# Gathering a chunk's decay rows on ScalarE and moving them by DMA, in a gated linear attention fused with a maxout layer

## The chip, the cores and the metric

The kernel runs on one core of a Trainium2 chip. The core has a matrix engine (TensorE, PE in the profile), VectorE (DVE), ScalarE (ACT), GpSimd (POOL) and SyncE (SP), which here only issues DMA transfers. Each engine works through its own instruction list in order; they meet through semaphores. The metric is the device time of one execution in microseconds (us), median of several runs.

## What is computed

Two stages, one after the other. The first is a recurrence per batch entry and head with a state of 48x48 and a decay per state row; the second is a maxout layer on its output.

```
B, H, S, D = q.shape                      # 4, 8, 768, 48
f = 1.0 / (1.0 + np.exp(-f_logit))
state = np.zeros((B, H, D, D)); y = np.zeros_like(q)
for t in range(S):
    state = f[:, :, t, :, None] * state + np.einsum('bhd,bhe->bhde', k[:, :, t], v[:, :, t])
    y[:, :, t] = np.einsum('bhd,bhde->bhe', q[:, :, t], state)
x = y.transpose(0, 2, 1, 3).reshape(B * S, H * D)          # 3072 x 384
out = np.maximum(x @ w1, x @ w2) @ w_out                   # d_ff = 1024
```

All inputs and the output are float32 in HBM.

## The kernel before

The sequence is cut into 6 chunks of 128 positions. A *tile* is one chunk of one batch entry with all 8 heads, 128 positions by 384 columns; there are 24, and tile `i` is chunk `i // 4` of batch entry `i % 4`. Within a chunk the recurrence is written with cumulative sums of the log decay: with `ell = log(1 + exp(-f_logit))`, a matmul with an upper triangular matrix gives `cum`, the sum of `ell` from the chunk's start to each position (L214). Then `ei = exp(cum)` scales k into `kp` (L237, VectorE), `ed = exp(-cum)` scales q into `qp` (L242, GpSimd). The scores of a chunk are `qp` times `kp`, masked (`a`, `am`); the output `y` of a tile is the state of the chunk before, multiplied by `qp` (L307), plus the scores times v (L312).

The state of the next chunk is `(state + sum of kp times v)`, times the decay over the whole chunk. The sum is the matmul `sa` (L281), `tmp` adds the old state on VectorE (L289), and `st` multiplies with the decay on GpSimd (L296), as two instructions of 64 partitions, one for the even heads (partitions 0 to 63), one for the odd (64 to 127). Heads are handled in 4 pairs; a head takes 48 of its 64 partitions.

The decay over the chunk, `fl`, must lie along the *partitions* of the state, whereas `cum` has the positions on its partitions and the head's rows along its columns. So the kernel before sums `ell` once more, with `ell` as the stationary operand: four matmuls, one per pair of heads, of 128x1 with a column of ones (L216), into columns 384 to 387 of the same PSUM tile. `a_fl` (L232) is a ScalarE activation of 128x4 that gives `fl = exp(-sum)`. The last chunk hands no state on and leaves out L216, `fl`, `sa`, `tmp` and `st`.

The second stage: `y` is copied to `x` (L317), transposed (`xT`), and with `d = x @ (w1 - w2)` in two halves (`d0`, `d1`, L334) and `g = relu(d)` in two halves (`g0`, `g1`, L341, called `gT`), the output is `o = x @ (w2 @ w_out) + g @ w_out`, as `o0` (6 of the 11 matmuls) and `o1` (the other 5) at L352. Of `o1`, the first matmul needs the first half of `g`, the four others the second half. `ob` evicts it and `out` stores it.

Every instruction's place is written out by hand in three strings of words "operation, tile": a prologue, a step that is repeated, and an epilogue. In a step for tile `i` the number is added to `i`:

```
st -4  d0 -1  cum 1  a 0  ed 1  d1 -1  g0 -1  am 0  lv 2  qp 1  fl 1  ei 1  lq 3  g1 -1
o0 -1  kpv 1  y 0  tmp -2  lk 3  o1 -1  x 0  e 2  xT 0  tr 1  ln 2  out -4  xTe 0  sa -1
tre 1  ob -1  lf 4  v 1
```

The order on one engine is the order of its words. So in the step of tile 12 GpSimd does `st` of tile 8 and then `qp` of tile 13; ScalarE does `ed`, `g0`, `fl`, `ei`, `g1`, `x`, `e`, `ln`; SyncE issues the loads `lv` 14, `lq` 15, `lk` 15, the store `out` 8 and the load `lf` 16. All DMA transfers are issued by SyncE and go into one queue. Each of the loads `lf`, `lk`, `lq`, `lv` (L148) fetches 192 KB as 1024 pieces of 192 bytes, into one of 9 buffers for its kind. `y` of tile 12 reads the state that `st` of tile 8 has written. `tmp` has two buffers, `fl` has five; `cum`, `tr`, `sa`, `y` and `xT` share three PSUM buffers.

The functions that the change touches:

Of the kernel before, what the change touches and what calls it, by code (L numbers as in the profile page):

```python
# [10 lines left out]
F32 = mybir.dt.float32  # L11
BF16 = mybir.dt.bfloat16
AF = mybir.ActivationFunctionType
# [25 lines left out]
"""  # L39

STEP = """
st -4  d0 -1  cum 1  a 0  ed 1  d1 -1  g0 -1  am 0  lv 2  qp 1  fl 1  ei 1  lq 3  g1 -1
o0 -1  kpv 1  y 0  tmp -2  lk 3  o1 -1  x 0  e 2  xT 0  tr 1  ln 2  out -4  xTe 0  sa -1
tre 1  ob -1  lf 4  v 1
"""
FIRST_STEP = 7
EPILOGUE = """
st 15  d0 18  cum 20  a 19  ed 20  d1 18  g0 18  am 19  qp 20  ei 20  lv 21  g1 18  o0 18
tmp 17  st 16  out 15  y 19  kpv 20  o1 18  x 19  lk 22  e 21  xT 19  tr 20  ln 21  xTe 19
# [14 lines left out]
def kernel(  # L64
# [13 lines left out]
    nc = tc.nc  # L78
    B, H, S, D = q.shape
    C = 128  # L80
    nch = S // C
    dm = H * D
# [3 lines left out]
    DP = 64  # L86
    NP = H // 2
# [3 lines left out]
    consts = ctx.enter_context(tc.tile_pool(name="consts", bufs=1))  # L91
    loads = ctx.enter_context(tc.tile_pool(name="loads", bufs=9))
    work = ctx.enter_context(tc.tile_pool(name="work", bufs=2))
# [8 lines left out]
    qp_b = [consts.tile([C, H, DP], BF16, name=f"qp{n}") for n in range(NQ)]  # L102
    kp_b = [consts.tile([C, H, DP], BF16, name=f"kp{n}") for n in range(NQ)]
    ell_b = [consts.tile([C, H, DP], BF16, name=f"ell{n}") for n in range(2)]
    st_b = [[consts.tile([C, NP, 2 * D], BF16, name=f"st{b}_{n}") for n in range(2)] for b in range(B)]
    ut = consts.tile([C, C], BF16)
    ident = consts.tile([C, C], BF16)
    ones_col = consts.tile([C, 1], BF16)
# [10 lines left out]
    def setup(n):  # L119
        if n == 0:  # L120
            for t in ell_b:
                nc.vector.memset(t, 0.0)
            nc.vector.memset(ones_col, 1.0)
            make_upper_triangular(nc, ut, 1.0, diag=True)
            make_identity(nc, ident)
            for t in (kp_b[0], qp_b[0]):
                nc.vector.memset(t, 0.0)
        elif n == 1:
            nc.vector.tensor_copy(mask, ut.unsqueeze(1).to_broadcast([C, H, C]))
            for t in kp_b[1:] + qp_b[1:]:  # L130
                nc.vector.memset(t, 0.0)
        else:
            for b in range(B):
                for t in st_b[b]:
                    nc.gpsimd.memset(t, 0.0)
# [3 lines left out]
    st = {}  # L139
# [37 lines left out]
    psum = {}  # L177
# [33 lines left out]
    def p_cum(i):  # L211
        ell = st[i]["ell"]
        ps = psum["cum", i] = ps_s.tile([C, 512], F32, name="cum", tag="s")
        nc.tensor.matmul(out=ps[:, 0:dm], lhsT=ut, rhs=ell[:, :, 0:D], start=True, stop=True)  # L214
        for p in range(NP if i // B < nch - 1 else 0):
            nc.tensor.matmul(out=ps[:, dm + p:dm + p + 1],  # L216
                             lhsT=ell[:, 2 * p:2 * p + 2, :].rearrange("p h d -> p (h d)"),
                             rhs=ones_col, start=True, stop=True)
# [7 lines left out]
        nc.scalar.activation(t, psum["cum", i][:, 0:dm], AF.Exp, scale=-1.0)  # L226

    def a_fl(i):
        if i // B == nch - 1:
            return  # L230
        t = st[i]["fl"] = work.tile([C, NP], F32, name="fl", tag="fl", bufs=5)
        nc.scalar.activation(t, psum["cum", i][:, dm:dm + NP], AF.Exp, scale=-1.0)  # L232

    def m_kp(i, eng):
        s = st[i]
# [55 lines left out]
    def m_st(i):  # L291
        c, b = divmod(i, B)
        if c < nch - 1:
            for o in range(2):
                r, e = slice(o * DP, (o + 1) * DP), slice(o * D, (o + 1) * D)
                nc.gpsimd.tensor_mul(st_b[b][(c + 1) % 2][r, :, e], st[i]["tmp"][r, :, e],  # L296
                                     st[i]["fl"][r, :].unsqueeze(2).to_broadcast([DP, NP, D]))

    def p_y(i):
        c, b = divmod(i, B)  # L300
# [36 lines left out]
    def a_g(i, half):  # L337
        s = st[i]
        if half == 0:
            s["g"] = work.tile([C, FG, C], BF16, name="gT", tag="gT", bufs=3)  # L340
        nc.scalar.activation(s["g"][:, half * 4:half * 4 + 4, :], psum.pop(("d", half, i)), AF.Relu)  # L341

    def p_o(i, half):
        s = st[i]
        if half == 0:
            psum["o", i] = ps_m.tile([C, dm], F32, name="o", tag="mm")
        mms = [(s["xT"][:, j, :], w2o[:, j, :]) for j in range(JG)]
        mms += [(lambda f=f: s["g"][:, f, :], wo[:, f, :]) for f in range(FG)]
        cut = 6
        for n in (range(0, cut) if half == 0 else range(cut, len(mms))):  # L350
            l, r = mms[n]
            nc.tensor.matmul(out=psum["o", i], lhsT=l() if callable(l) else l, rhs=r,  # L352
                             start=(n == 0), stop=(n == len(mms) - 1))
# [22 lines left out]
    def ob_last(h):  # L376
        t = st[T - 1]["ob", h] = consts.tile([C, dm // 2], F32, name=f"obl{h}")
        if h == 0:
            nc.scalar.copy(t, psum.pop(("last", h)))
        else:  # L380
            nc.vector.tensor_copy(t, psum.pop(("last", h)))
# [5 lines left out]
    def warm(n):  # L387
# [5 lines left out]

    ops = {
        "setup": setup, "lf": lambda i: load(i, "f"), "lk": lambda i: load(i, "k"),
        "lq": lambda i: load(i, "q"), "lv": lambda i: load(i, "v"),
        "lw1": lambda n: load_w(w1_f, moe_w1, n), "lw2": lambda n: load_w(w2_f, moe_w2, n), "lwo": load_wo,
        "w2c": cast_w2, "w2ca": lambda j: cast_w2(j, True), "woc": cast_wo,
        "wd": sub_wd, "wdp": lambda j: sub_wd(j, nc.gpsimd),
        "w2T": tr_w2, "w2Te": ev_w2T, "w2o": mm_w2o, "w2oe": ev_w2o,  # L400
        "e": a_e, "ln": a_ln, "v": v_v, "cum": p_cum, "ei": a_ei, "ed": a_ed, "fl": a_fl,
        "kp": lambda i: m_kp(i, nc.gpsimd), "kpv": lambda i: m_kp(i, nc.vector),
        "qp": lambda i: m_qp(i, nc.gpsimd), "qpv": lambda i: m_qp(i, nc.vector),
        "tr": lambda i: p_tr(i, "kq"), "trk": lambda i: p_tr(i, "k"), "trq": lambda i: p_tr(i, "q"),
        "tre": lambda i: v_tr(i, "kq"), "trke": lambda i: v_tr(i, "k"), "trqe": lambda i: v_tr(i, "q"),
        "a": p_a, "am": v_am, "sa": p_sa, "tmp": v_tmp, "st": m_st,
        "y": p_y, "x": a_x, "xT": p_xT, "xTe": v_xT,
        "d0": lambda i: p_d(i, 0), "d1": lambda i: p_d(i, 1),
        "g0": lambda i: a_g(i, 0), "g1": lambda i: a_g(i, 1),
        "o0": lambda i: p_o(i, 0), "o1": lambda i: p_o(i, 1), "ob": v_ob, "out": store, "warm": warm,  # L410
        "lo": p_last, "lob0": lambda n: ob_last(0), "lob1": lambda n: ob_last(1),
        "lout": store_last,
    }
# [4 lines left out]
    def run(op, n):  # L418
        key = (same.get(op, op), n)
        if op == "warm" or key not in done:  # L420
            done.add(key)
            ops[op](n)

    def pairs(text):
        words = text.split()
        return [(op, int(n)) for op, n in zip(words[0::2], words[1::2])]

    for op, n in pairs(PROLOGUE):
        run(op, n)
    last = pairs(EPILOGUE)  # L430
    kept = split_up | {(same.get(op, op), n) for op, n in last}
    for i in range(FIRST_STEP, T + 8):
        for op, n in pairs(STEP):
# [34 lines left out]
```

## Time and profile before

| | |
|---|---|
| median of 8 runs | 146.2 us (145.91 to 149.46) |
| profiled execution | 146.55 us |
| its span (first to last instruction) | 144.8 us |
| mean granted TensorE clock | 0.987 of full speed |
| L216 matmuls, 80 of 128x1 | 4.9 us busy, mean 165 ns |
| L232 `fl`, 20 of 128x4 | 3.7 us busy, mean 183 ns |
| L222 `ei`, 24 of 128x384 | 12.1 us busy, mean 504 ns |
| L296 `st`, 40 of 64x192 | 25.2 us busy, mean 630 ns |
| DMA packets | 104612, 28.60 MB, mean 198 GB/s |
| packets under 512 bytes | 100368 |

The profile is of one execution. An instruction's time is from its start to its end; the next one of the engine may start before that end, so the sum of the means is more than the busy time, and the distance of two starts says what an instruction takes from its engine. The span is what the profile covers; the time of the execution has something more around it. "Chain" means the work that ended last, followed back from the end, at each step to what released it. For a DMA two things are shown: when SyncE's issuing instruction ran, and how long after its start the data had landed.

### The profile page before, as it was taken

The page shows a single profiled execution, that of the slowest core. Times are in us where ns is not written, and L with a number is a line of the kernel's source. Part 1 is how long each engine was busy: PE and PEld are TensorE (multiplying, and loading weights), DVE is VectorE, ACT ScalarE, POOL GpSimd, SP SyncE. Part 2 cuts the span into 40 slices and gives each one's busy share as a digit, 9 for nine tenths or more (in the row PEclk, how much of TensorE's full clock was granted, in tenths as well). Part 3 has the DMA queues.
Part 4 walks back from the last instruction along what each step waited for, and adds up shares of the span by engine and source line. Part 5 has one row for each costly group of instructions (what it writes and reads, how often), then busy time and mean ns, then how long its engine had stood idle before and what let it go on. Part 6 is the DMA issues. An engine that isn't in the chain of part 4 may idle for free.

```text
span 144.8 us, 4442 instructions
## 1 busy us (share of the span) xinstructions
PE 131.1 (91%) x1820; PEld 102.1 (71%) x1820; DVE 106.7 (74%) x191; ACT 88.4 (61%) x199; POOL 53.9 (37%) x80
## 2 busy tenths in 40 slices
PE   0196499999999999999999999999999999999981
PEld 0034357688678878887887788788878877777771
DVE  7834875796798779777977887797779778986520
ACT  3572545967577575758666775857586667664430
POOL 8220060220547055246425633652464255252000
PEclk9999959999999999999999999999999999999999
DMA  4999999799898999989999999999899798971111
GB/s 97 257 359 386 342 292 193 141 199 182 174 184 154 196 189 226 200 185 201 185 228 194 226 208 198 232 186 210 181 214 229 147 255 180 235 212 59 58 56 54
DMA packets 104612, 28.60 MB, mean 198 GB/s; under 512 B 100368, under 2 KB 103568, under 8 KB 104592
## 3 DMA queue, kind: packets, MB, share of 16 engines
q1 hardware_dynamic: 104592, 28.32, 94.2%
q8 instruction: 14, 0.23, 0.8%
q14 instruction: 6, 0.05, 0.1%
HBM read 23.59 MB, written 4.72 MB: 196 GB/s over the span
## 4 chain that ended last, share of the span: by engine, by line
PE 71%; SPq 20%; DMA 4%; issue 1%; DVE 1%; POOL 1%; ACT 0%; POOLq 0%
PE o L352 25%; PE d L334 21%; SPq L148 14%; PE tr L249 6%; PE a L267 5%; SPq L153 4%; DMA qt<-in_q_dram 4%; PE y L312 3%; PE y L307 2%; PE xtp L322 2%; PE cum L214 2%; PE sa L281 2%; SPq L157 2%; PE o L373 1%; PE cum L216 1%
## 5 line engine op out<-in xcount | busy, mean ns | idle before, releaser
L242 POOL TENSOR_TENSOR qp<-qt,ed 128x384 bf16<-128x384 f32 x22 | 22.0, 1001 | 62.5 <-ACT ed L226 32.5
L334 PE MATMUL d<-xT,wd 128*128 128x128 bf16 x576 | 40.4, 220 | 0.5 <-DVE xT L326 0.4
L352 PE MATMUL o<-wo,gT 128*128 128x384 bf16 x184 | 37.4, 325 | 0.0
L334 PEld LDWEIGHTS <-wd 128*128 128x128 bf16 x576 | 34.4, 114 | 3.3 <-issue 0.6
L341 ACT ACTIVATE gT<-d 128x512 bf16<-128x512 f32 x48 | 29.1, 606 | 10.0 <-PE d L334 9.8
L272 DVE TENSOR_TENSOR am<-a,mask 128x1024 bf16<-128x1024 f32 x24 | 29.4, 1224 | 0.6 <-PE a L267 0.5
L296 POOL TENSOR_TENSOR st<-tmp,fl 64x192 bf16<-64x192 f32 x40 | 25.2, 630 | 1.6
L326 DVE COPY xT<-xtp 128x384 bf16<-128x384 bf16 x24 | 8.6, 357 | 20.2 <-PE xtp L322 20.2
L352 PEld LDWEIGHTS <-gT 128*128 128x128 bf16 x184 | 16.1, 97 | 9.0 <-ACT gT L341 0.2
L226 ACT ACTIVATE ed<-cum 128x384 f32<-128x384 f32 x24 | 11.8, 492 | 17.1 <-PE cum L216 13.7
L258 DVE COPY trs<-tr 128x1024 bf16<-128x1024 bf16 (+1 forms) x27 | 16.9, 631 | 4.6 <-PE tr L249 2.8
L317 ACT CAST x<-y 128x384 bf16<-128x384 f32 x24 | 11.5, 478 | 11.6 <-PE y L312 11.5
L237 DVE TENSOR_TENSOR kp<-kt,ei 128x384 bf16<-128x384 f32 x23 | 14.7, 639 | 0.9 <-POOL qp L242 0.5
L352 PE MATMUL o<-w2o,xT 128*128 128x384 bf16 x69 | 15.0, 326 | 0.0
L201 ACT ACTIVATE e<-ft 128x384 f32<-128x384 f32 x24 | 12.5, 526 | 2.8 <-DMA ft<-in_f_logit_dram 2.8
L214 PE MATMUL cum<-ell,ut 128*128 128x384 bf16 x24 | 8.1, 339 | 6.7 <-ACT ell L205 6.7
L205 ACT ACTIVATE ell<-e 128x384 bf16<-128x384 f32 x24 | 12.5, 524 | 0.7
L357 DVE COPY ob<-o 128x384 f32<-128x384 f32 x23 | 12.6, 548 | 0.0
L222 ACT ACTIVATE ei<-cum 128x384 f32<-128x384 f32 x24 | 12.1, 504 | 0.0
L312 PE MATMUL y<-vb,am 128*128 128x48 bf16 x192 | 11.2, 183 | 0.2 <-DVE vb L209 0.2
L312 PEld LDWEIGHTS <-am 128*128 128x128 bf16 x192 | 9.7, 96 | 2.3 <-DVE am L272 0.4
L289 DVE TENSOR_TENSOR tmp<-sa,st 128x384 f32<-128x384 f32 x20 | 10.9, 546 | 0.0
(56 smaller groups left out, 171.7 us busy)
## 6 DMA issues: line engine op xcount, KB each, us to landing
ft<-in_f_logit_dram SPq DMA_DIRECT2D x24, 192.0 KB, 4.4
qt<-in_q_dram SPq DMA_DIRECT2D x24, 192.0 KB, 4.6
kt<-in_k_dram SPq DMA_DIRECT2D x24, 192.0 KB, 4.6
vt<-in_v_dram SPq DMA_DIRECT2D x24, 192.0 KB, 4.3
out_dram<-ob SPq DMA_DIRECT2D x23, 192.0 KB, 3.8
w_f<-in_moe_w_dram SPq DMA_DIRECT2D x6, 512.0 KB, 7.0
wo_f<-in_moe_w_out_dram SPq DMA_DIRECT2D x2, 768.0 KB, 8.4
out_dram<-obl SPq DMA_DIRECT2D x2, 96.0 KB, 1.6
```

The costliest lines, as they stand in the source:

```text
L148: nc.sync.dma_start(out=t, in_=SRC[name][b, :, sl, :].rearrange("h p d -> p h d"))
L201: nc.scalar.activation(e, ld[i]["f"].rearrange("p h d -> p (h d)"), AF.Exp, scale=-1.0)
L237: eng.tensor_mul(s["kp"][:, :, 0:D], ld[i]["k"], s["ei"].rearrange("p (h d) -> p h d", h=H))
L242: eng.tensor_mul(s["qp"][:, :, 0:D], ld[i]["q"], s["ed"].rearrange("p (h d) -> p h d", h=H))
L258: nc.vector.tensor_copy(s["tr"][:, n:n + len(sel)], psum.pop(("tr" + sel, i)))
L272: nc.vector.tensor_mul(am.rearrange("p o n c -> p (o n) c"), psum.pop(("a", i)).rearrange("p o n c -> p (o n) c"), mask)
L296: nc.gpsimd.tensor_mul(st_b[b][(c + 1) % 2][r, :, e], st[i]["tmp"][r, :, e], st[i]["fl"][r, :].unsqueeze(2).to_broadcast([DP, NP, D]))
L312: nc.tensor.matmul(out=y[:, ds], lhsT=am[:, o, p, :], rhs=vb[:, ds], start=(c == 0), stop=(c == 0 or o == 1))
L334: nc.tensor.matmul(out=ps[:, n, :], lhsT=wd[:, j, ff(f)], rhs=st[i]["xT"][:, j, :], start=(j == 0), stop=(j == JG - 1))
L341: nc.scalar.activation(s["g"][:, half * 4:half * 4 + 4, :], psum.pop(("d", half, i)), AF.Relu)
L352: nc.tensor.matmul(out=psum["o", i], lhsT=l() if callable(l) else l, rhs=r, start=(n == 0), stop=(n == len(mms) - 1))
L357: nc.vector.tensor_copy(t, psum.pop(("o", i)))
```

## The change

From chunk 2 on (tiles 8 to 19; the last chunk has no `fl`), the four 128x1 matmuls of a tile are left out. The total over the chunk is the last row of `cum`, position 127. ScalarE's activation now reads partitions 96 to 127 of `cum`, all 384 columns, in the order (even or odd head, row in the head, pair), which puts neighbours 96 elements apart, and writes into a tile `row` that collects the four batch entries of a chunk. Only partition 127 of it is used. After the fourth tile, two DMA copies, one for the even heads and one for the odd, take this one partition's 768 values each to 48 partitions of 16 values (64 bytes) of a tile `fl_b`. There are two tiles of each kind, used by chunks in turn. In chunks 0 and 1 the matmuls stay, and the activation writes `fl_b` directly. `st` reads `fl_b`. The two `fl_b` tiles are set to zero at the start on VectorE.

The copies are a new word `fd`, the first of a step, which does something in the steps of tiles 11, 15 and 19. In SyncE's order each pair of copies stands between the load `lf` of the step before (tile 14, 18, 22) and the load `lv` of its own step (tile 13, 17, 21).

```diff
 STEP = """
-st -4  d0 -1  cum 1  a 0  ed 1  d1 -1  g0 -1  am 0  lv 2  qp 1  fl 1  ei 1  lq 3  g1 -1
+fd 0  st -4  d0 -1  cum 1  a 0  ed 1  d1 -1  g0 -1  am 0  lv 2  qp 1  fl 1  ei 1  lq 3  g1 -1
...
+FIRST_MOVED = 2
...
+    row_b = [consts.tile([C, 2, D, B, NP], F32, name=f"row{n}") for n in range(2)]
+    fl_b = [consts.tile([C, B, NP], F32, name=f"fl{n}") for n in range(2)]
...
-            for t in kp_b[1:] + qp_b[1:]:
+            for t in kp_b[1:] + qp_b[1:] + fl_b:
                 nc.vector.memset(t, 0.0)
...
-        for p in range(NP if i // B < nch - 1 else 0):
+        for p in range(NP if i // B < FIRST_MOVED else 0):
             nc.tensor.matmul(out=ps[:, dm + p:dm + p + 1],
...
     def a_fl(i):
-        if i // B == nch - 1:
-            return
-        t = st[i]["fl"] = work.tile([C, NP], F32, name="fl", tag="fl", bufs=5)
-        nc.scalar.activation(t, psum["cum", i][:, dm:dm + NP], AF.Exp, scale=-1.0)
+        c, b = divmod(i, B)
+        if c < FIRST_MOVED:
+            nc.scalar.activation(fl_b[c % 2][:, b, :], psum["cum", i][:, dm:dm + NP], AF.Exp, scale=-1.0)
+        elif c < nch - 1:
+
+            nc.scalar.activation(row_b[c % 2][96:C, :, :, b, :], psum["cum", i][96:C, 0:dm].rearrange(
+                "t (p h d) -> t h d p", p=NP, h=2), AF.Exp, scale=-1.0)
+
+    def move_fl(i):
+        c, b = divmod(i, B)
+        if FIRST_MOVED <= c < nch - 1 and b == B - 1:
+            for h in range(2):
+                nc.sync.dma_start(out=fl_b[c % 2][h * DP:h * DP + D].rearrange("d b p -> d (b p)"),
+                                  in_=row_b[c % 2][C - 1:C, h].rearrange("o d b p -> o d (b p)"))
...
-                                     st[i]["fl"][r, :].unsqueeze(2).to_broadcast([DP, NP, D]))
+                                     fl_b[c % 2][r, b, :].unsqueeze(2).to_broadcast([DP, NP, D]))
```

More of the change, by code (lines that the diff above doesn't have):

```diff
@@ L409 @@
         "g0": lambda i: a_g(i, 0), "g1": lambda i: a_g(i, 1),
-        "o0": lambda i: p_o(i, 0), "o1": lambda i: p_o(i, 1), "ob": v_ob, "out": store, "warm": warm,
+        "fd": move_fl, "o0": lambda i: p_o(i, 0), "o1": lambda i: p_o(i, 1), "ob": v_ob, "out": store, "warm": warm,
         "lo": p_last, "lob0": lambda n: ob_last(0), "lob1": lambda n: ob_last(1),
```

## The prediction

> **What bounds the kernel now.** I read the busy shares first, then the chain of waits for the middle of the run, then each engine's order of time inside one step, and last the DMA issues.
>
> ```profile
> PE 131.1 (91%) x1820; PEld 102.1 (71%) x1820; DVE 106.7 (74%) x191; ACT 88.4 (61%) x199; POOL 53.9 (37%) x80
> PE 71%; SPq 20%; DMA 4%; issue 1%; DVE 1%; POOL 1%; ACT 0%; POOLq 0%
> 40.00:110.00 70.00, 70.00 (x1060) 57.12 (x1059) 56.15 (x100) 46.92 (x112) 31.54 (x42) 1.00 1.07 200
> ```
>
> The second line is the chain's share by engine, the third the stretch 40 to 110 us (mean, then PE, PEld, DVE, ACT, POOL busy, granted clock, DMA share, GB/s). TensorE is busy for all 70 us at the full clock; until 36.6 us the chain is the loading of weights and first tiles. After that the time is the sum of what TensorE executes. But the DMA engines are as full (share 1.07): what is late in the DMA queue stays late.
>
> Two pieces of the chain (start, length, what), a middle step and the first step of the last chunk, which has no state to hand on and so lacks the 128x1 matmuls of L216 already:
>
> ```profile
> 79.86 0.16 PE cum L214
> 80.02 0.08 PE cum L216 x4
> 80.10 0.33 PE a L267 x8
> ...
> 84.84 0.16 PE cum L214
> ```
>
> ```profile
> 114.70 0.16 PE cum L214
> 114.86 0.33 PE a L267 x8
> ...
> 119.60 0.16 PE cum L214
> ```
>
> With the four matmuls a step takes 84.84-79.86 = 4.98 us, without them 119.60-114.70 = 4.90. Their worth on the chain is 0.08 us, not the 4x165 ns that their group's mean would suggest, since matmuls overlap.
>
> ScalarE in the step of tile 12 (start, length):
>
> ```profile
> 80.14 0.49 ACT L226 ACTIVATE ed<-cum 128x384 f32<-128x384 f32 x1 [1.05 <-PE cum L216]
> 80.53 0.59 ACT L341 ACTIVATE gT<-d 128x512 bf16<-128x512 f32 x1
> 81.00 0.18 ACT L232 ACTIVATE fl<-cum 128x4 f32<-128x4 f32 x1
> 81.05 0.51 ACT L222 ACTIVATE ei<-cum 128x384 f32<-128x384 f32 x1
> 81.42 0.63 ACT L341 ACTIVATE gT<-d 128x512 bf16<-128x512 f32 x1
> 82.61 0.48 ACT L317 CAST x<-y 128x384 bf16<-128x384 f32 x1 [0.55 <-PE y L312]
> ```
>
> Instructions overlap: from `fl` to the next start only 0.05 us pass, after a 128x384 Exp 0.37. ScalarE idles 0.55 and 1.05 us per step.
>
> GpSimd, and SyncE's queue, around the state update of tile 8 (`st` pair at 76.75), the first that will read a moved row:
>
> ```profile
> 76.75 1.39 POOL L296 TENSOR_TENSOR st<-tmp,fl 64x192 bf16<-64x192 f32 x2
> 80.76 1.01 POOL L242 TENSOR_TENSOR qp<-qt,ed 128x384 bf16<-128x384 f32 x1 [2.62 <-ACT ed L226]
> ```
>
> ```profile
> 75.42 1.57 SPq L362 DMA_DIRECT2D out_dram<-ob  x1
> 77.08 0.73 SPq L148 DMA_DIRECT2D ft<-in_f_logit_dram  x1
> 77.87 0.64 SPq L148 DMA_DIRECT2D vt<-in_v_dram  x1
> ```
>
> ```profile
> ft<-in_f_logit_dram SPq DMA_DIRECT2D x1, 192.0 KB, 3.3
> ```
>
> The last is the DMA view of 77.0 to 77.5 us: this load (tile 14) lands 3.3 us after its issue, at 80.4. SyncE issues one transfer after the other with hardly a gap and is some three tiles behind what could be stored. That is what the moved rows meet.
>
> **The change, part by part.** *Matmuls.* Tiles 8 to 19 lose four 128x1 matmuls each with their weight loads: 12 x 0.08 = 0.96 us off the chain. Bounds: 0 if something else paces the step, 0.96 as the last chunk shows.
>
> *ScalarE.* Twelve 128x4 activations become 32x384 ones. They take the place of `fl`, between the first `gT` and `ei`; no row shows such a read (four elements 384 bytes apart in PSUM). Nearest below is the contiguous 128x384 Exp from the same tile, 0.37 us from start to start; above, the 128x768 cast of L172, 0.83 us, as if each element took two turns. I take 0.37: width sets these rows, and the `ell` row, which leaves gaps in its output, costs what `e` does (524 against 526 ns). So `ei`, the second `gT` and `kp` come 0.32 us later. `kp` (VectorE) has 0.94 us of idle time before `xT` behind it, `x` has 0.55 before it. The second `gT` is the tight one. From the start of `cum` it ends at 0.37 (last chunk, 114.53 to 114.90) + 0.39 + 0.47 + 0.37 + 0.37 + 0.63 = 2.60 us. TensorE's second half of `o` starts 82.41-79.70-0.08 = 2.63 after `cum`; its second matmul, first to need that tile, 0.16 later; the weight load before it takes 0.10, the hand-over some 0.05. So 2.64 is the limit: 0.04 us of room. This part costs nothing up to 0.41 us from start to start; above that, each excess is paid twelve times.
>
> The Trainium skill (Advanced Engine Details and Errata, Memory Cachelines) speaks against this read: PSUM lines hold two FP32 values, and pairs should be adjacent for best throughput. It says so of matmuls; no run here shows it for ScalarE. Taken at double cost it would be the upper bound above, with the time of rival 2.
>
> *The rows' way.* Six copies, two behind the last tile of chunks 2, 3 and 4. In SyncE's order each pair stands between the `ft` load of tile 14 (18, 22) and the `vt` load of tile 13 (17, 21). They need the activation of tile 11 (near 71 us) and GpSimd's reads two chunks earlier, both long done at 77.8, so the queue doesn't stop. But a copy lands only behind what was queued before. Lower bound: with that `ft` load; upper: like a load of its own, 4.6 us after issue (median for `qt`), 82.5. In between: five transfers pass per 4.98 us step, about 1.0 each; 96 pieces against a load's 1024 are 0.1 us, with 0.05 of hand-over 0.15 per pair. This delays every later load as well, by 0.15, 0.30, 0.45; `ft` of tile 14 landed 2.6 us ahead of its reader (82.98), so loads stay hidden, and if they were not, 0.45 would be paid.
>
> Landing: 80.4+0.15 = 80.55; 96.30+3.0+0.30 = 99.6; 115.62+3.9+0.45 = 119.95 (issue and time to landing of the `ft` loads of tiles 14, 18, 22). The `st` pair that needs the row has stood ready since 76.75; it now waits, and takes 1.40 + 0.05. The next tile's `y` (L307) needs the new state; it started at 82.04, 101.94 and 121.69, and comes earlier by the matmuls gone ahead of it (6, 10, 12 x 0.08 = 0.48, 0.80, 0.96):
> - tile 12: state at 82.00, wanted at 81.56: wait 0.44.
> - tile 16: state at 101.05, wanted at 101.14+0.44: none.
> - tile 20: state at 121.40, wanted at 120.73+0.44 = 121.17: wait 0.23.
>
> Together 0.67, bounds 0 and, with every row landing 1.9 us later, 2.6. Behind the waiting `st` on GpSimd stands `qp` of the next tile: it ends 1.0 us after the pair, its transpose comes 1.57 after `y`, so it is never later than `y` makes it. VectorE's `tmp` of tile 10 waits for the same pair (two buffers) and has the 0.94 us of idle time.
>
> The Trainium skill (DMA: Bandwidth & Descriptors, Rules for kernel authors) calls transfers under 64 KB mostly overhead, and puts a DMA's fixed part at about 2 us. By that alone the first row would land at 79.9, in time, and 0.96 would stay. The trace's loads of 3.0 to 3.9 us say that the queue ahead decides.
>
> *The rest.* Two memsets of 16 columns on VectorE, 0.06 each by the `ones_col` row, lie in the first microseconds, where the chain is on the loads; uncovered, 0.12. `st` reads the same shape from another tile: nothing.
>
> **Sum.** 144.8 - 0.96 + 0.67 = 144.5 us of span. The profiled execution took 146.55, with 1.75 outside the span, and lies 0.35 above the median of 146.2; I put the change against the median: 146.2 - 0.29 = 145.9.
>
> **Rivals.**
> 1. *The rows come in time.* The queue's lag against TensorE wanders: the `ft` load's landing is 0.7 us after `cum` of its step for tile 14 and 0.3 before it for tile 18 (99.3 against 99.60). With a lag smaller by 0.5 no `y` waits: 146.2 - 0.96 = 145.2. Against it: full DMA engines.
> 2. *ScalarE's strided read is slow; slower than before.* Place: second `gT`, each of 12 steps. It decides from 0.41 us start to start; at 0.49 the 0.08 gained is spent, at 0.74 (double) each step pays 0.33-0.08 = 0.25, 12 x 0.25 = 3.0: 149.2, while `y` no longer waits for rows. For it: room of only 0.04; against: all ScalarE rows go by element count.
> 3. *The rows land like loads*, 1.9 us later: waits reach 2.6, 146.2 - 0.96 + 2.6 = 147.8. It decides (slower than before) from 0.3 us beyond my landing times. For it: no such copy is in the trace; against: little data, same queue.
> 4. The change not doing what it says: the copies are six and the matmuls 48 fewer in its instruction order; I give it no time.
>
> **How the numbers follow.** Forecast (145.5 to 146.3) 0.40, rival 1 0.20, rival 2 0.20, rival 3 0.20. 0.3% is 0.44 us, about what a measurement of this kernel can tell: faster is below 145.76, slower above 146.64. The forecast's 0.40 divides 0.16 faster, 0.21 same, 0.03 slower; rival 1: 0.19 and 0.01 same; rival 2: 0.05 same, 0.15 slower; rival 3: 0.05 same, 0.15 slower. Sum 0.35, 0.32, 0.33. Range: 145.2, all gain kept, to 147.8, rival 3; what lies beyond is most of rival 2's upper half.
>
> **What the profile after would show.** Steps of 4.90 us from tile 8 on; the new activation 0.37 to 0.41 us from start to start, and no TensorE wait in front of L352's second part (rival 2: one in each step). GpSimd's `st` waiting on a DMA three times, landing near 80.6, 99.6, 120; TensorE waiting on `st` once or twice, in all below 1 us (rival 1 none, rival 3 over 2). Wrong it would be above all if the copies' landing isn't set by the loads ahead of them, or if the step is not TensorE's sum.

## The result, and the profile after

The changed kernel takes 147.8 us (median of 11 runs; 146.2 before). The ratio is 1.0105, 95% interval 1.0081 to 1.0128: some 1.5 us slower, where 0.3 us faster was forecast. The time, 147.79 us, lies on the very upper end of the range, 147.8, and on the other side of no change. That end was rival 3's time, a loss by late rows, which didn't happen here; that the measured time falls on it is chance. The profiled execution's span went from 144.8 to 146.0 us.

Of the page after, busy times and two groups (line, engine, operation, tiles, form, count | busy, mean ns | idle before, released by):

```profile
PE 132.1 (90%) x1772; PEld 99.8 (68%) x1772; DVE 106.8 (73%) x193; ACT 93.6 (64%) x199; POOL 53.3 (36%) x80
L310 POOL TENSOR_TENSOR st<-tmp,fl 64x192 bf16<-64x192 f32 x40 | 24.5, 612 | 5.8 <-DMA fl<-row 3.4
L366 PEld LDWEIGHTS <-gT 128*128 128x128 bf16 x184 | 16.1, 97 | 11.2 <-ACT gT L355 3.1
```

TensorE executes 48 matmuls fewer and is a little longer busy. GpSimd's `st` now waits for the copies, 3.4 us in all. New is the last line's end: the weight loads of `o` wait 3.1 us for the second half of `gT`, 12 times about 0.26.

One step in the chain of waits (start, length, what):

```profile
80.35 0.16 PE cum L218
80.52 0.33 PE a L281 x8
...
82.98 0.17 PE o L366
83.15 0.01 issue
83.16 0.82 PE o L366 x4
...
85.43 0.16 PE cum L218
```

The four small matmuls are gone between `cum` and `a`. But the step takes 85.43-80.35 = 5.08 us, not 4.98 as before and not 4.90. The chain breaks after the first matmul of `o`'s second part, exactly where the second half of `gT` is first needed: the next matmul starts 0.33 us after the first in each of the twelve steps, where it started 0.16 after it before. The five matmuls of this part take 0.17+0.01+0.82 = 1.00 us on the chain, where they took 0.81 before:

```profile
82.57 0.81 PE o L352 x5
```

ScalarE in this step of the changed kernel:

```profile
80.61 0.49 ACT L230 ACTIVATE ed<-cum 128x384 f32<-128x384 f32 x1 [1.22 <-PE cum L218]
81.00 0.59 ACT L355 ACTIVATE gT<-d 128x512 bf16<-128x512 f32 x1
81.61 0.48 ACT L238 ACTIVATE row<-cum 32x384 f32<-32x384 f32 x1
82.12 0.49 ACT L226 ACTIVATE ei<-cum 128x384 f32<-128x384 f32 x1
82.51 0.59 ACT L355 ACTIVATE gT<-d 128x512 bf16<-128x512 f32 x1
83.02 0.48 ACT L331 CAST x<-y 128x384 bf16<-128x384 f32 x1
```

The new activation is not slow by itself: 0.48 us, like `ei`. But it starts 0.61 us after the `gT` before it, where `fl` started 0.47 after, and `ei` starts 0.51 after it, where `ei`, of the same width, is followed after 0.37 to 0.39. It overlaps with neither neighbour. The first `gT` to `ei` took 0.52 us before and takes 1.12 now, 0.60 more, where the prediction had 0.32.

GpSimd, around the first row that was moved:

```profile
76.16 1.00 POOL L256 TENSOR_TENSOR qp<-qt,ed 128x384 bf16<-128x384 f32 x1 [2.75 <-issue]
79.93 1.08 POOL L310 TENSOR_TENSOR st<-tmp,fl 64x192 bf16<-64x192 f32 x2 [2.77 <-DMA fl<-row]
81.23 1.00 POOL L256 TENSOR_TENSOR qp<-qt,ed 128x384 bf16<-128x384 f32 x1 [0.23 <-POOL st L310]
```

`st` waits 2.77 us for the copy, as foretold. It is done at 81.0, though, and the `y` that needs the state starts at 82.45: in this kernel the wait costs `y` nothing. Twelve steps of 4.98 us became steps of 5.08 (one of them 5.14): 12 x 0.10 = 1.2 us, the whole difference of the spans. The medians differ by 0.35 us more, because the profiled execution of before lay that much above its median.

### The profile page after: what moved, and what is told of

Same layout as the page of the kernel before. It is cut to its first block, busy times and chain, and to the rows that moved or that the text cites. A ratio compares the mean times of both kernels' runs of the same rounds, so it can differ in the third digit from the quotient of the medians.

```text
span 146.0 us, 4364 instructions
## 1 busy us (share of the span) xinstructions
PE 132.1 (90%) x1772; PEld 99.8 (68%) x1772; DVE 106.8 (73%) x193; ACT 93.6 (64%) x199; POOL 53.3 (36%) x80
## 4 chain that ended last, share of the span: by engine, by line
PE 85%; DMA 6%; SPq 5%; ACT 1%; issue 1%; DVE 0%
PE o L366 30%; PE d L348 24%; PE tr L263 7%; DMA wo_f<-in_moe_w_out_dram 6%; PE a L281 5%; PE w2op L196 4%; PE y L326 3%; PE xtp L336 3%; PE cum L218 3%; PE y L321 2%; PE sa L295 2%; SPq L152 2%; SPq L157 2%; SPq L161 1%; ACT wo L176 1%; PE o L387 1%
## 5 line engine op out<-in xcount | busy, mean ns | idle before, releaser
L366 PE MATMUL o<-wo,gT 128*128 128x384 bf16 x184 | 39.4, 326 | 0.1
L355 ACT ACTIVATE gT<-d 128x512 bf16<-128x512 f32 x48 | 28.6, 596 | 9.7 <-PE d L348 9.5
L310 POOL TENSOR_TENSOR st<-tmp,fl 64x192 bf16<-64x192 f32 x40 | 24.5, 612 | 5.8 <-DMA fl<-row 3.4
```

## The experiments

**Which part costs: the activation or the copies?** Theory A, from the trace above: the activation. Theory B: the rows' way through the queue. First the copies were left out.

```diff
-        if FIRST_MOVED <= c < nch - 1 and b == B - 1:
+        if False and FIRST_MOVED <= c < nch - 1 and b == B - 1:
```

> The six copies are left out; the state update reads what chunks 0 and 1 left in the rows' tile. Everything else is the changed kernel. Theory A (ScalarE: the 32x384 activation makes the second gT late by 0.60 us, and TensorE waits about 0.17 us in each of 12 steps): time stays at 1.010 to 1.011 of before, steps of 5.08 us. Theory B (the copies cost it, by GpSimd's waits for them and their place in the queue): the time falls to 0.994 to 1.000 of before, steps of 4.90 us.

Ratio to before 1.0106 (1.0053 to 1.0158), as with the copies, and twelve steps of 5.08 us. The interval is wide, but the steps agree: in the changed kernel the copies cost nothing that can be measured, beyond 0.06 us in its one step of 5.14.

Then the other way round, the activations left out:

```diff
-        elif c < nch - 1:
+        elif False and c < nch - 1:
...
+            for t in row_b:
+                nc.gpsimd.memset(t[96:C], 0.5)
```

> The 32x384 activations of tiles 8 to 19 are left out (the row tile is set once, by GpSimd at the start); the copies and the missing matmuls stay. Theory A: steps of 4.90 us, 12 x 0.08 = 0.96 us below before, and up to 0.7 back where y waits for a row: 0.993 to 0.998 of before. Theory B: stays at 1.010. GpSimd's memsets lie in the first 10 us, where it waits for loads; if they show, it is up to 1 us.

0.9982 (0.9956 to 1.0008): on the upper edge of A's range, and B is out. All steps from tile 8 on take 4.90 us except two, with 5.53 and 5.19. Those are the late rows that the prediction was about. The chain across the first of them:

```profile
97.27 2.54 DMA fl<-row
99.81 0.02 issue
99.83 0.02 POOLq L312
99.85 0.09 issue
99.94 0.51 POOL st L312
100.45 0.07 issue
100.52 0.72 POOL st L312
101.23 0.04 issue
101.28 0.20 PE y L323
```

The reader sees the path worked out in the prediction: the copy lands at 99.81, the two halves of `st` follow, then `y` at 101.28. So the rows do cost something as soon as the step is fast: 0.63 and 0.29 us here (of the 0.29, the wait of `y` is 0.13; the rest goes the way shown at f1 below). The longer step of the changed kernel had covered it.

**Mending the place.** If the second `gT` is what is late, the activation can stand behind it; and if rows are late, the copies can be issued earlier.

```diff
-fd 0  st -4  ...  am 0  lv 2  qp 1  fl 1  ei 1  lq 3  g1 -1
+fd 0  st -4  ...  am 0  lv 2  qp 1  ei 1  lq 3  g1 -1  fl 1
```

> The activation stands behind the second gT in ScalarE's order instead of in front of ei. Theory A: the second gT is in time again, the activation falls into ScalarE's 0.55 us idle time before x: steps of 4.90 us, 0.993 to 0.998 of before, the upper end if y waits for rows. Rival A2 (ScalarE's longer work costs wherever it stands, x is late instead): steps above 4.95, 1.000 or more. Theory B: stays at 1.010.

0.9951 (0.9910 to 0.9992): faster than before, though by little more than the interval, with the new activation still in all twelve steps. Rival A2 is out; steps of 4.90 us, apart from three of 6.02, 5.44 and 5.26, in which `y` waits for `st`, and `st` for a copy. These came to 2.0 us in the profiled execution, which took 147.6 us, 1.1 more than the median of its runs; 0.7 at most was expected. How late the queue runs differs from one execution to the next. Then also the copies earlier:

```diff
-fd 0  st -4  ...  lq 3  g1 -1  fl 1
+st -4  ...  lq 3  g1 -1  fl 1  fd 1
```

> As the run before, and the copies are issued three transfers earlier, in the step in which the fourth activation runs (between the lq and lk loads). If y waits for late rows in the run before, that is gone here: 0.993 to 0.994 of before, and faster than the run before by as much as y waited there (up to 0.7 us). If the rows come in time there too, the two are the same. Should SyncE now wait for the activation, loads come later; they have 2.6 us in hand, so no change from that.

0.9912 (0.9879 to 0.9945), a little better than expected (0.993 to 0.994 lies inside the interval), and the lowest ratio of all kernels run. Every step from tile 8 on took 4.90 us in its trace. The intervals of this run and the one before overlap, so the 0.4% between them is not settled by their times; the steps of the two traces show that `y` waits in the one and not in the other. The early issue has a price that this trace shows: SyncE waited 4.1 us for the activation of tile 11 before it issued the first pair, and from 74 to 78 us the DMA engines were busy for 0.05 of the time or less. The loads behind came later, yet no step was longer for it. In g2, the other run with the early issue, SyncE waited for no activation at this place.

**What takes the overlap away?** Four variants of the activation, one execution each, read from their steps and starts and not from their times. First all 128 partitions instead of 32, with the same order of elements:

```diff
-            nc.scalar.activation(row_b[c % 2][96:C, :, :, b, :], psum["cum", i][96:C, 0:dm].rearrange(
+            nc.scalar.activation(row_b[c % 2][0:C, :, :, b, :], psum["cum", i][0:C, 0:dm].rearrange(
```

> The changed kernel, whose new activation works on all 128 partitions instead of 96 to 127, with the same order of elements. In the changed kernel the activation starts 0.61 us after the gT before it and ei 0.51 after it, where 128x384 instructions overlap by some 0.13 us (0.47 and 0.37). If the 32 partitions or their start at 96 take the overlap away, it is 0.47 and 0.37 here and the step 4.95 us or less; if the order of elements does, 0.61 and 0.51 again and the step 5.08.

ScalarE in a step of this kernel:

```profile
64.37 0.59 ACT L355 ACTIVATE gT<-d 128x512 bf16<-128x512 f32 x1
64.85 0.50 ACT L238 ACTIVATE row<-cum 128x384 f32<-128x384 f32 x1
65.22 0.51 ACT L226 ACTIVATE ei<-cum 128x384 f32<-128x384 f32 x1
65.59 0.63 ACT L355 ACTIVATE gT<-d 128x512 bf16<-128x512 f32 x1
66.39 0.48 ACT L331 CAST x<-y 128x384 bf16<-128x384 f32 x1 [0.17 <-PE y L326]
```

The overlap is back on both sides, 0.48 and 0.37 us, though the instruction does four times the work. It is the partitions, not the order of elements.

Steps are 4.90 us, with two of 5.33 and 5.04. In these two `y` doesn't wait: it starts 2.26 us after `cum`, as in every step of 4.90. GpSimd, VectorE and TensorE's weight loads in the first of them:

```profile
79.19 1.08 POOL L310 TENSOR_TENSOR st<-tmp,fl 64x192 bf16<-64x192 f32 x2 [3.78 <-DMA fl<-row]
80.35 1.00 POOL L256 TENSOR_TENSOR qp<-qt,ed 128x384 bf16<-128x384 f32 x1
80.46 1.31 DVE L251 TENSOR_TENSOR kp<-kt,ei 128x384 bf16<-128x384 f32 x1 [0.28 <-ACT ei L226]
81.69 0.54 DVE L303 TENSOR_TENSOR tmp<-sa,st 128x384 f32<-128x384 f32 x1
82.28 0.23 PEld L263 LDWEIGHTS <-kp 128*128 128x128 bf16 x4 [0.42 <-DVE tmp L303]
```

`st` waits for the copy, `qp` stands behind it and now runs beside `kp`, which takes 1.31 us, where it takes 0.56 to 0.73 in the steps around; `tmp` ends later, and the transposes (`tr`) wait 0.42 us for it. In all 14 cases of this trace after 50 us in which GpSimd was at an instruction when `kp` began, `kp` ended 0.41 to 0.42 us after that instruction's end; alone it took 0.55 to 0.56. It looks as if `kp` went on only when GpSimd was done; no run tests this by itself. So a late row can cost by this way too.

The next three agree on the partitions. They change the pattern on the 32 partitions, in the kernel without copies (in short form):

```diff
-row_b[c % 2][96:C, :, :, b, :]  <-  cum[96:C].rearrange("t (p h d) -> t h d p", p=NP, h=2)
+row_flat[96:C, b]               <-  cum[96:C, 0:dm]                                         # f2
+row_flat[96:C, b]               <-  cum[96:C].rearrange("t (p h d) -> t h d p", p=NP, h=2)  # f3
+row_b[c % 2][96:C, :, :, b, :]  <-  cum[96:C].rearrange("t (h d p) -> t h d p", h=2, p=NP)  # f4
```

> The kernel without copies, whose activation reads partitions 96 to 127 in the order in which they lie and writes them so (the rows' order is left out). If the order of elements takes the overlap away: 0.47 and 0.37 us, second gT 0.28 earlier, step 4.90. If the partitions do: 0.61 and 0.51, step 5.08.

> The kernel without copies; the activation reads PSUM with a distance of 96 elements as in the changed kernel and writes without gaps. If the strided read of PSUM takes the overlap: 0.61 and 0.51, step 5.08. If the gaps in the output do: 0.47 and 0.37, step 4.90. A slower stream would show in the activation's own duration, 0.48 so far.

> The kernel without copies; the activation reads PSUM in order and writes in groups of four with gaps as in the changed kernel. The mirror of the run before: overlap back (0.47 and 0.37, step 4.90) if the strided read takes it, gone (0.61 and 0.51, step 5.08) if the gaps in the output do. If it is the number of dimensions of the pattern, both this run and the one before lose it.

In all three the activation starts 0.61 us after `gT`, `ei` 0.51 after it, its own 0.48 us are unchanged, and the twelve steps take 5.08 us. A read with a distance of 96 elements, or gaps in the output, cost nothing here.

**Number of partitions, or where they start?** The same activation on partitions 0 to 31, and on 64 to 127 (kernels without copies, one execution each):

```diff
-            nc.scalar.activation(row_b[c % 2][96:C, :, :, b, :], psum["cum", i][96:C, 0:dm].rearrange(
+            nc.scalar.activation(row_b[c % 2][0:32, :, :, b, :], psum["cum", i][0:32, 0:dm].rearrange(     # g3
+            nc.scalar.activation(row_b[c % 2][64:C, :, :, b, :], psum["cum", i][64:C, 0:dm].rearrange(     # g4
```

> The kernel without copies, whose activation takes partitions 0 to 31 (wrong rows) instead of 96 to 127. If the number of partitions takes the overlap away: 0.61 and 0.51 us around it, step 5.08. If it is the start at 96: 0.47 and 0.37, step 4.90.

> The kernel without copies, whose activation takes partitions 64 to 127. If any set of partitions other than the neighbours' loses the overlap: 0.61 and 0.51, step 5.08. If the loss depends on how many are left out, it lies between that and 0.47 and 0.37.

On partitions 0 to 31:

```profile
69.59 0.59 ACT L355 ACTIVATE gT<-d 128x512 bf16<-128x512 f32 x1
70.06 0.47 ACT L238 ACTIVATE row<-cum 32x384 f32<-32x384 f32 x1
70.43 0.47 ACT L226 ACTIVATE ei<-cum 128x384 f32<-128x384 f32 x1
70.80 0.58 ACT L355 ACTIVATE gT<-d 128x512 bf16<-128x512 f32 x1
```

On partitions 64 to 127:

```profile
70.70 0.59 ACT L355 ACTIVATE gT<-d 128x512 bf16<-128x512 f32 x1
71.31 0.48 ACT L238 ACTIVATE row<-cum 64x384 f32<-64x384 f32 x1
71.82 0.49 ACT L226 ACTIVATE ei<-cum 128x384 f32<-128x384 f32 x1
72.21 0.59 ACT L355 ACTIVATE gT<-d 128x512 bf16<-128x512 f32 x1
```

Thirty-two partitions from 0 overlap with 128 from 0 (0.47, 0.37; steps 4.90). Sixty-four from 64 don't (0.61, 0.51; steps 5.08). What loses the overlap is where the partitions start, not their count: a start at 0 keeps it, a start at 64 or 96 loses it, beside neighbours that start at 0. Whether two instructions that both start at 96 would overlap with each other wasn't tried, so whether a start other than 0 or a start other than the neighbours' is the cause stays open. So does whether it is the read or the write, whose first partitions were moved together.

**Is that the whole loss?** The kernel of f1 timed, and once more with the copies issued early.

> The kernel of f1 again (the new activation on all 128 partitions, order and copies as in the changed kernel), now timed. If the lost overlap on ScalarE is the whole loss of the changed kernel: steps of 4.90 us, 0.96 us gained, 0.3 to 0.9 given back where y waits for a row: 0.994 to 0.999 of before. If the changed kernel loses in another way as well: above 1.000.

0.9991 (0.9969 to 1.0013): the loss is gone, and nothing gained. Steps of 4.90 us, but three are 0.9, 1.2 and 0.4 us longer for late rows in the profiled execution, in all more than what the matmuls saved. That execution took 147.9 us, 1.7 above the median of its runs; by the ratio the runs gave back about 0.8 us (an estimate: 0.96 less 0.0009 x 146), as expected.

> As the run before, with the copies issued in the step of the fourth activation, between the lq and lk loads. No y should wait: every step 4.90 us, 0.993 to 0.994 of before, 0.3 to 0.9 us less than the run before. If the rows still come late, the two agree.

0.9957 (0.9920 to 0.9994); the ratio is a little above what was expected, 0.993 lies inside the interval. Span 143.4 us, every step from tile 8 on 4.90. GpSimd around the three state updates that read a first row:

```profile
76.43 1.27 POOL L310 TENSOR_TENSOR st<-tmp,fl 64x192 bf16<-64x192 f32 x2 [0.37 <-DMA fl<-row]
...
97.47 1.08 POOL L310 TENSOR_TENSOR st<-tmp,fl 64x192 bf16<-64x192 f32 x2 [1.81 <-DMA fl<-row]
...
116.99 1.08 POOL L310 TENSOR_TENSOR st<-tmp,fl 64x192 bf16<-64x192 f32 x2 [1.73 <-DMA fl<-row]
```

`st` still waits for the copies, up to 1.8 us, but is done well before its `y`. Issued three transfers earlier, the rows come in time. Its interval and that of g1 overlap too; the steps decide, of one execution each.

## Why the prediction was wrong, point by point

- **The chain and the gain.** TensorE sets the time from about 40 us on, and the four matmuls are worth 0.08 us per step: right. Wherever ScalarE was in time and no row was late, steps took 4.90 us. It is no more than 0.08 because the `a` behind `cum` then waits for VectorE's transposed tiles; the trace after has that wait 12 times in the twelve steps, 2.5 us in all, and the last chunk of before has it too (4 times, 0.8 us).
- **"I take 0.37": the step that failed.** The prediction found the tight place (the second `gT`), and said that each excess over 0.41 us is paid twelve times. But it took the new activation's price from the row of a full-width Exp and counted the overlap with both neighbours as given. Measured are 0.51 us behind it and 0.14 more in front, 0.65 by the same count. This is between its bounds, 0.37 and 0.83, and nearer to the upper one; the lower was taken. By "width sets these rows" 0.37 was the right price for an activation that starts at partition 0 (f1, g3); that the start at 96 could matter was nowhere in the sum.
- **Rival 2 had the place and the sign, and the wrong cause.** The strided read is not slow (f2, f3, f4). Its price per step was also off. By its own count 0.65-0.41-0.08 = 0.16 net per step, 1.9 us; measured were 0.10 and 1.2. The limit was drawn 0.1 too early: it put the whole weight load and 0.05 of hand-over between the tile and the matmul, 0.15 in all. The trace after has the tile done at 83.10, the load start at 83.15 and the chain the matmul at 83.16, 0.06 behind the tile, and so in each of the twelve steps. The prediction also has two prices for a doubled read, 0.83 as the bound and 0.74 in the rival.
- **The Trainium skill's PSUM line rule** (Advanced Engine Details and Errata, Memory Cachelines), weighed there as the case against the change: on ScalarE the runs show nothing of it. A read whose neighbours are 96 elements apart took 0.48 us (f3), the contiguous one 0.48 (f2).
- **The rows' way.** That copies land behind the loads ahead of them, that `st` waits for them, and that `y` is at stake: right. In 14 of the 15 pairs issued at the old place the first copy landed 0.15 to 0.21 us behind the load ahead of it (0.15 was taken for the pair; once it was 1.66). Foretold for 4.90 us steps were 0.67 us of waits of `y`, bounds 0 and 2.6; found were 0.77 (e2), none (f1), 1.9 (e3) and 2.5 (g1), and with the way by `kp` 0.92, 0.57, 2.0 and 2.6. f1 and g1 are the same kernel: the size is a matter of how late the queue happens to run in an execution. In the changed kernel itself it was hidden, since ScalarE had made the step longer, as rival 2 said.
- **The 2 us fixed part of the Trainium skill** (DMA: Bandwidth & Descriptors, Latency and other measured facts): the copies of 3 KB landed 3.3 to 4.8 us after their issue in the trace after, and 2.1 to 4.5 in g2. The first pair of e4, issued when the load ahead had already landed, took 1.8 and 1.7 us, near the page's figure. With loads ahead the queue decides, as taken.
- **Memsets and loads behind the copies:** nothing of these shows in any step.
- **`qp` and `tmp` behind the waiting `st`:** put at nothing, and wrong in that. The prediction held `qp` against `y` and left `kp`'s duration as it was. In f1 `kp` took 1.31 and 1.01 us beside the late `qp`, and the whole 0.57 us came this way; 0.15 us did in the third long step of e2, e3 and g1, and 0.06 in one step of the changed kernel, where `kp` took 0.86 us.

## What to carry to other kernels

An engine that is 61% busy can still have one instruction on which the bound engine waits within hundredths of a microsecond: before work is moved there, find what stands behind the new instruction, and by how much it may be late. Price the new instruction by the distance of starts on both of its sides, not by its duration; here an instruction on 32 partitions cost more than one on all 128. And a wait that is hidden in one version comes back when another part gets faster: the copies, almost free in the changed kernel, took nearly the whole gain as soon as ScalarE was mended, and had to be issued earlier.

## What the runs showed of the hardware

- ScalarE activations that start at partition 0 overlap with their neighbours by 0.12 to 0.13 us on each side (128x384 Exp: 0.37 us from start to start at 0.50 us duration, f1), also when one has 32 partitions and the next 128 (g3). One that starts at partition 64 (g4) or 96 (e1, f2 to f4) between neighbours that start at 0 loses this on both sides: 0.61 instead of 0.47 us before it, 0.51 instead of 0.37 behind it. Taking all 128 partitions was faster than the 32 that were needed.
- A ScalarE read of PSUM with 384 bytes between elements (f3) took as long as one without gaps (f2), 0.48 us for 32x384.
- A 128x384 matmul's weight load and the matmul itself started within 0.01 us of each other when the weights came last (83.15 and 83.16 in the trace after, and so in all twelve steps).
- A 128x384 product of VectorE (`kp`) took 0.55 to 0.56 us alone. Where it began while GpSimd's `qp` or `st` was running, it ended 0.41 to 0.42 us after that one's end in all 14 cases of f1 after 50 us, and so took up to 1.31 us.
